# Operand tiles of a fused attention and two-FFN kernel begin 64 bytes further on than the weights' tiles

## The chip, the cores and the metric

One core of a Trainium2 chip runs one program. The metric is the device time of one execution in microseconds (us). The kernel before takes 951.75 us, the median of three runs (951.35 to 951.98).

## What is computed

```
scores = (q @ k^T) / sqrt(64) - log(448)        # 4 batches x 12 heads, 448 x 448 each, float32
attn   = sigmoid(scores) @ v
x      = attn, heads side by side               # 1792 tokens x 768
x      = (relu(x @ w_in)**2) @ w_out            # 768 -> 2048 -> 768
h      = x @ w_in2
out    = (h * sigmoid(1.702 * h)) @ w_out2      # 768 -> 2048 -> 768
```

All inputs and the output are float32.

## The kernel before, in words

There are two parts. In the first (until about 128 us) TensorE makes the scores of 24 pairs of heads and multiplies their sigmoids with v. Meanwhile ACT, DVE and the queue of POOL decode the four weight matrices: a step loads a raw block (`RAW`), turns it into float32 (`DEC`), adds and subtracts its quarters and writes seven blocks to DRAM (`scr`). Some of these steps are left to the second part, between its other work.

In the second part two token halves pass through the two FFNs: eight stages (`STAGES`), four of the kind "in" (`plan_in`) and four of the kind "out" (`plan_out`). Each stage is one Strassen-like product with seven partial products of eight units each, so 56 units. A unit is nine matmuls of 128 x 128 weights against 128 x 448 operand columns: three tiles in each of three passes, because a float32 factor is split into a high part that is rounded to fp32r and the low rest. The passes are high x high, high x low and low x high, lines 475 to 477. So the second part has 8 x 56 x 9 = 4032 matmuls, and each loads its own weights.

The weights of two units come by SP's queue into an `LD` tile; ACT copies its high part into an `SL` tile (named s), DVE subtracts to get the low part beside it. The operand of a partial product lies in a `T` tile (named t): `Operand` has ACT write the high half and DVE the low half. X, tmp and the four h tiles hold the matrices from which operands are made. The order on every engine is fixed when the program is built, by a planner (`settle`, `run`) with costs and due times of its own; a unit of TensorE counts there as `UNIT_US` = 1.8225 us.

The tiles of a pool lie one behind the other in SBUF, in the order in which they are asked for. Before the change this order is X (4 tiles of 5376 bytes in each partition), T (5 of 10752), LD (4 of 3072), SL (3 of 6144), tmp (5376), RAW (2 of 12288), DEC (2 of 6144), and then those of the attention (rq, qh, ql, rv, a, al, xst, bias, half), in whose place the h and sig tiles lie later. All sizes as far as the sig tiles, bias and half apart, are multiples of 256 bytes. So are all the offsets at which matmuls read within a tile: 512 bytes from one block of 128 weight columns to the next, 1536 and 3072 between the parts of an SL tile, 1792 and 5376 in a T tile. So the operand and the weights of every matmul of the second part begin at the same remainder of 256.

Of the kernel before, what the change touches and what calls it, by code (L numbers as in the profile page):

```python
# [9 lines left out]
F32R = mybir.dt.float32r  # L10
# [6 lines left out]
B, H, S, D = 4, 12, 448, 64  # L17
DM, DFF = 768, 2048
P = 128
# [10 lines left out]
NK = 3  # L30
# [5 lines left out]
NT = 5  # L36
# [42 lines left out]

PACE = (6, 6, 5, 1, 4, 5, 5)  # L80


@with_exitstack
def sigmoid_attention_two_ffn(ctx: ExitStack, tc: tile.TileContext, qk, v, w, outT):
# [13 lines left out]

    cpool = ctx.enter_context(tc.tile_pool(name="cpool", bufs=1))
    X = [[cpool.tile([P, NK, S], F32, name=f"xq{i}{j}") for j in range(2)] for i in range(2)]  # L100
    T = [cpool.tile([P, 2, NK, S], F32R, name=f"t{n}") for n in range(NT)]
    LD = [cpool.tile([P, 2, W], F32, name=f"ld{n}") for n in range(NLOAD)]
    SL = [cpool.tile([P, 2, 2, W], F32R, name=f"s{n}") for n in range(NSLOT)]
    tmp = cpool.tile([P, NK, S], F32, name="tmp")
    RAW = [cpool.tile([P, 4 * W, 2], U32, name=f"raw{n}") for n in range(2)]
    DEC = [cpool.tile([P, 4, W], F32, name=f"dec{n}") for n in range(2)]
# [30 lines left out]
    def act(fn, n, keys=(), after=(), extra=0.0, **kw):  # L137
        return Node("act", fn, 0.115 + extra + 0.833e-3 * n, keys, after, 0.105, **kw)
# [4 lines left out]
    def move(eng, out, in_, size, keys=(), after=(), **kw):  # L143

        def go():
            eng.dma_start(out() if callable(out) else out, in_() if callable(in_) else in_)

        n = Node("sp" if eng is nc.sync else "pool", go, 0.45 if eng is nc.sync else 0.55, keys, after, DMA_US + size / 250e3, **kw)
        n.size = size
        return n  # L150

    def activation(out, in_, fn=AF.Copy, **kw):
        nc.scalar.activation(out, in_, fn, **kw)  # L153
# [9 lines left out]
    def att_order():  # L163
        for u in range(NHP // 2 + 1):
            if u:
                yield from (("V", hp, c) for hp in (2 * u - 2, 2 * u - 1) for c in range(NFULL))
                yield ("VL", u - 1, 0)
            if u < NHP // 2:
                todo = [("S", hp, c) for hp in (2 * u, 2 * u + 1) for c in range(NFULL)]
                todo.insert(0 if u else NFULL, ("SL", u, 0))  # L170
                yield from todo
# [3 lines left out]
    def make_steps():  # L175
        kind = "L"
        us = {"S": SCORES_US, "V": VALUES_US, "VL": LEFT_US, "SL": LEFT_US}
        for key in att_order():
            new = "L" if key[0] in ("VL", "SL") else key[0]
            t = us["V" if key in WHOLE else key[0]]  # L180
# [61 lines left out]
    def load_qk(hp):  # L242
        if hp > 1:
            n = move(nc.sync, RQ[hp % 4], qk[hp], P * 2 * S * 4, (), [pe.get(("SL", (hp - 4) // 2, 0)), split.get(hp - 4)], part=0)
            rq_load[hp] = n, n
# [29 lines left out]
    def next_two():  # L275
        turn[0] += 1
        b = 2 * (turn[0] % 4)
        return b, mem["ps"][:, b : b + 2]
# [28 lines left out]
    def scores_left(u):  # L307
        b, ps = next_two()
        step = pe["SL", u, 0]

# [90 lines left out]
    class Operand:  # L401

        def __init__(self, src, n, keys, first, last):
# [3 lines left out]
            free_t[i] = last  # L407
            self.t = t = T[i]
            keys = [("T", i), *keys]
            act(lambda: activation(t[:, 0, : src().shape[1]], src()), n * S, keys, [units[old]] if old >= 0 else ())  # L410
# [38 lines left out]
    def plan_weights():  # L449
        for q in range(len(STAGES) * UNITS // 2):  # L450
            m, io, _ = STAGES[2 * q // UNITS]
            us = [ORDER[io][(2 * q + i) % UNITS] for i in range(2)]
            t, sl = LD[q % NLOAD], SL[q % NSLOT]
            ld = ("LD", q % NLOAD)
# [414 lines left out]
```

## Time and profile before

| | |
|---|---|
| median of three runs | 951.75 us |
| the profiled execution | 950.77 us |
| its span, first to last instruction | 949.0 us |
| matmuls in the second part | 4032 |
| first and last start of these | 128.06 and 945.09 us |
| granted TensorE clock | 1.00 throughout |

The page of the profile gives each engine's busy time, the chain of work that ended last, and the costliest groups of instructions by line. PE is TensorE's matmuls, PEld its weight loads. Matmuls overlap in their records: one is recorded from the time it starts until its last result is out, while the next has already started, so durations add up to more than the time. What a matmul costs is the distance from its start to the next one's.

### The profile page before, as it was taken

The numbers are of one execution on the slowest core, as the hardware profiler recorded it, in microseconds if no ns is written. First come the engines' busy times: TensorE is split into PE (matmuls) and PEld (weight loads), VectorE is DVE, ScalarE is ACT, GpSimd is POOL, SyncE is SP. The second block draws the span as 40 slices with busy tenths as digits, with TensorE's granted clock in tenths as the row PEclk, the third lists the DMA queues.
The fourth block names the chain that finished last, engine by engine and source line by source line (L and its number), as shares of the span: only waits on it lengthen the run. The fifth ranks groups of instructions, "written<-read, shape, count | busy, mean of one in ns | idle before, by whom it ended". The sixth has DMA issues, their size and how long they took to land.

```text
span 949.0 us, 13696 instructions
## 1 busy us (share of the span) xinstructions
PE 944.6 (100%) x4949; PEld 822.8 (87%) x4949; DVE 809.3 (85%) x839; ACT 604.6 (64%) x715; POOL 53.5 (6%) x100
## 2 busy tenths in 40 slices
PE   9999999999999999999999999999999999999998
PEld 4555479999999999999999999999999999999997
DVE  3989986699877999999999987999989999778662
ACT  6788776778868775555464666657684646445551
POOL 0110100000000000000000000000000000000000
PEclk9999999999999999999999999999999999999999
DMA  8899989999886766896567699877975448754341
GB/s 340 301 335 356 335 293 332 324 354 334 290 324 227 250 231 212 317 364 216 161 243 286 202 359 325 312 247 251 351 279 171 133 146 288 261 166 132 115 137 58
DMA packets 98627, 245.75 MB, mean 259 GB/s; under 512 B 10752, under 2 KB 72960, under 8 KB 94464
## 3 DMA queue, kind: packets, MB, share of 16 engines
q1 hardware_dynamic: 84736, 150.51, 46.5%
q0 software_dynamic: 13824, 94.38, 27.2%
q8 instruction: 38, 0.62, 0.3%
q14 instruction: 29, 0.24, 0.1%
HBM read 175.11 MB, written 69.73 MB: 258 GB/s over the span
## 4 chain that ended last, share of the span: by engine, by line
PE 100%; ACT 0%; issue 0%
PE ps L475 29%; PE ps L476 29%; PE ps L477 29%; PE ps L332 6%; PE ps L298 5%; PE ps L346 1%; PE ps L317 1%; PE ps L790 0%; PE ps L293 0%; ACT xq L635 0%; PE ps L471 0%
## 5 line engine op out<-in xcount | busy, mean ns | idle before, releaser
L475 PE MATMUL ps<-t,s 128*128 128x448 f32 x1344 | 490.9, 365 | 0.0
L477 PE MATMUL ps<-t,s 128*128 128x448 f32 x1344 | 490.8, 365 | 0.0
L476 PE MATMUL ps<-t,s 128*128 128x448 f32 x1344 | 490.8, 365 | 0.0
L153 ACT ACTIVATE s<-ld 128x768 fp32r<-128x768 f32 x224 | 189.4, 846 | 249.4 <-PE ps L476 206.6
L477 PEld LDWEIGHTS ps<-t,s 128*128 128x128 f32 x1344 | 252.5, 188 | 19.9
L476 PEld LDWEIGHTS ps<-t,s 128*128 128x128 f32 x1344 | 252.5, 188 | 19.9
L475 PEld LDWEIGHTS ps<-t,s 128*128 128x128 f32 x1344 | 252.5, 188 | 19.9
L156 DVE TENSOR_TENSOR s<-ld,s 128x768 fp32r<-128x768 f32 x224 | 213.6, 954 | 61.7 <-ACT s L153 56.6
L156 DVE TENSOR_TENSOR t<-h,t 128x1344 fp32r<-128x1344 f32 (+1 forms) x72 | 100.4, 1397 | 8.8 <-ACT t L153 8.7
L153 ACT ACTIVATE t<-h 128x1344 fp32r<-128x1344 f32 (+1 forms) x72 | 85.6, 1190 | 4.4 <-DVE h L156 2.9
L153 ACT ACTIVATE h<-ps 128x448 f32<-128x448 f32 x112 | 59.8, 536 | 27.0 <-PE ps L477 26.8
L153 ACT ACTIVATE a<-ps,bias 128x896 f32<-128x896 f32 x72 | 66.1, 1023 | 3.2 <-PE ps L293 3.2
L332 PE MATMUL ps<-a,rv 128*64 128x448 f32 x288 | 56.8, 543 | 0.1
L217 DVE SCALAR_TENSOR_TENSOR dec<-raw,dec 128x1536 uint32<-128x1536 uint32 x32 | 56.2, 1755 | 0.5
L219 DVE SCALAR_TENSOR_TENSOR dec<-raw,dec 128x1536 uint32<-128x1536 uint32 x32 | 56.1, 1753 | 0.3
L153 ACT ACTIVATE dec<-raw 128x1536 f32<-128x1536 f32 x32 | 51.9, 1621 | 0.0
L156 DVE TENSOR_TENSOR h<-h,h 128x1344 f32<-128x1344 f32 (+1 forms) x36 | 50.0, 1397 | 1.0 <-DMA h<-hm 0.8
L153 ACT ACTIVATE h<-h 128x896 f32<-128x896 f32 x48 | 44.9, 945 | 4.8 <-DVE h L156 4.4
L332 PEld LDWEIGHTS ps<-a,rv 128*64 128x64 f32 x288 | 19.6, 137 | 32.4 <-issue 22.6
L213 DVE TENSOR_SCALAR dec<-dec 128x1536 f32<-128x1536 f32 x32 | 30.7, 959 | 15.6 <-ACT dec L153 15.6
L156 DVE TENSOR_TENSOR t<-xq,t 128x1344 fp32r<-128x1344 f32 x24 | 37.2, 1552 | 5.9 <-ACT t L153 5.4
L156 DVE TENSOR_TENSOR h<-ps,h 128x448 f32<-128x448 f32 x64 | 38.8, 619 | 2.8 <-PE ps L477 2.5
(58 smaller groups left out, 616.1 us busy)
## 6 DMA issues: line engine op xcount, KB each, us to landing
ld<-scr SPq DMA_DIRECT2D x448, 192.0 KB, 3.8
raw<-in_w POOLq DMA_DIRECT2D x32, 1536.0 KB, 8.2
scr<-dec POOLq DMA_DIRECT2D x32, 768.0 KB, 5.5
scr<-raw POOLq DMA_DIRECT2D x28, 576.0 KB, 6.2
hm<-h SPq DMA_DIRECT2D x32, 448.0 KB, 5.8
h<-hm SPq DMA_DIRECT2D x16, 672.0 KB, 5.4
rq<-in_qk SPq DMA_DIRECT2D x22, 448.0 KB, 8.2
rv<-in_v SPq DMA_DIRECT2D x12, 448.0 KB, 6.1
```

Source lines behind the costliest of these rows:

```text
L153: nc.scalar.activation(out, in_, fn, **kw)
L156: nc.vector.tensor_tensor(out=out, in0=in0, in1=in1, op=op)
L213: dve(lambda: nc.vector.tensor_scalar(out=d, in0=d, scalar1=LEAST, scalar2=LARGEST, op0=ALU.max, op1=ALU.min), 4 * W, [dk], each=0.52e-3)
L217: dve(lambda: nc.vector.scalar_tensor_tensor(out=u, in0=raw[:, :, 0], scalar=29, in1=u, op0=ALU.logical_shift_right, op1=ALU.bitwise_or), ...
L219: dve(lambda: nc.vector.scalar_tensor_tensor(out=u, in0=raw[:, :, 1], scalar=0x80000000, in1=u, op0=ALU.bitwise_and, op1=ALU.bitwise_or), ...
L298: nc.tensor.matmul(ps[:, j, :S], kk[rows, keys], qq[rows, QUERIES], start=(i == 0), stop=(i == 2))
L317: nc.tensor.matmul(ps[out, j, :S], r[rows, :LEFT], r[rows, QUERIES], start=True, stop=True)
L332: nc.tensor.matmul(ps[rows, :S], t[:, hp % 2 * NFULL + c, rows], a[:, j], start=(c == 0), stop=False)
L346: nc.tensor.matmul(mem["ps"][out, b + i, :S], t[rows, 2 * NFULL, out], AL[rows, j], start=False, stop=True)
L475: nc.tensor.matmul(o, sh[:, cols], t[:, 0, k], start=start, stop=False, skip_group_check=True)
L476: nc.tensor.matmul(o, sh[:, cols], t[:, 1, k], start=False, stop=False, skip_group_check=True)
L477: nc.tensor.matmul(o, lo[:, cols], t[:, 0, k], start=False, stop=stop, skip_group_check=True)
```

## The change

The LD and SL tiles are asked for ahead of the T tiles. The first T tile gets 16 elements (64 bytes) more than it needs, and its operand begins behind them; the other four follow it without a gap. Each T is then a view of the same shape as before. So X, LD and SL keep the remainder of 256 at which they began, and everything from T on (tmp, RAW, DEC, the attention's tiles, h and sig) begins 64 bytes further on by that measure. No instruction, wait or transfer is added, removed or given another size. The planner's costs stay as they are.

```diff
+APART = 16
+
...
     X = [[cpool.tile([P, NK, S], F32, name=f"xq{i}{j}") for j in range(2)] for i in range(2)]
-    T = [cpool.tile([P, 2, NK, S], F32R, name=f"t{n}") for n in range(NT)]
     LD = [cpool.tile([P, 2, W], F32, name=f"ld{n}") for n in range(NLOAD)]
     SL = [cpool.tile([P, 2, 2, W], F32R, name=f"s{n}") for n in range(NSLOT)]
+    T = []
+    for n in range(NT):
+        skip = 0 if n else APART
+        t = cpool.tile([P, skip + 2 * NK * S], F32R, name=f"t{n}")
+        T.append(t[:, skip:].rearrange("p (a k n) -> p a k n", a=2, k=NK))
     tmp = cpool.tile([P, NK, S], F32, name="tmp")
```

## Rows read from the trace of the kernel before

**Rows 1.** The page: busy us of each engine (share of the span) x instructions.
```profile
PE 944.6 (100%) x4949; PEld 822.8 (87%) x4949; DVE 809.3 (85%) x839; ACT 604.6 (64%) x715; POOL 53.5 (6%) x100
```
**Rows 2.** The page: granted TensorE clock, in tenths, in 40 slices of the span.
```profile
PEclk9999999999999999999999999999999999999999
```
**Rows 3.** The page: chain that ended last, share of the span by line.
```profile
PE ps L475 29%; PE ps L476 29%; PE ps L477 29%; PE ps L332 6%; PE ps L298 5%; PE ps L346 1%; PE ps L317 1%; PE ps L790 0%; PE ps L293 0%; ACT xq L635 0%; PE ps L471 0%
```
**Rows 4.** Waits of PE: engine, line, releaser: us in total, times, longest.
```profile
PE ps L790 <- PEq L858: 0.8, 1, 0.8
```
**Rows 5.** Stretches: length, busy us (x) of PE, PEld, DVE, ACT, POOL; clock, DMA share.
```profile
130.00:240.00 110.00, 110.00 (x544) 101.97 (x543) 91.52 (x101) 78.80 (x105) 8.81 (x17) 1.00 0.91 320
240.00:340.00 100.00, 100.00 (x495) 92.68 (x494) 84.19 (x94) 78.08 (x104) 9.17 (x17) 1.00 0.80 283
340.00:440.00 100.00, 100.00 (x495) 92.70 (x494) 96.92 (x90) 58.36 (x59) 3.20 (x6) 1.00 0.79 280
440.00:540.00 100.00, 100.00 (x495) 92.68 (x495) 95.15 (x91) 54.95 (x56) 6.13 (x11) 1.00 0.63 209
540.00:640.00 100.00, 100.00 (x495) 92.70 (x494) 89.33 (x100) 64.33 (x86) 7.00 (x14) 1.00 0.88 311
640.00:740.00 100.00, 100.00 (x496) 92.68 (x495) 93.93 (x108) 63.18 (x87) 7.60 (x13) 1.00 0.74 260
740.00:840.00 100.00, 100.00 (x495) 92.69 (x494) 90.35 (x81) 55.33 (x59) 0.00 (x0) 1.00 0.61 203
840.00:949.00 109.00, 105.46 (x521) 97.40 (x519) 62.87 (x55) 47.91 (x51) 0.00 (x0) 1.00 0.36 118
```
**Rows 6.** Timeline of PE: the first and the last matmul of the second part.
```profile
128.06 0.45 PE L475 MATMUL ps<-t,s 128*128 128x448 f32 x1
...
945.09 0.37 PE L477 MATMUL ps<-t,s 128*128 128x448 f32 x1
```
**Rows 7.** Timeline of PE: six matmuls in a row, from 299.8 us.
```profile
299.80 0.36 PE L476 MATMUL ps<-t,s 128*128 128x448 f32 x1
300.00 0.37 PE L477 MATMUL ps<-t,s 128*128 128x448 f32 x1
300.20 0.36 PE L475 MATMUL ps<-t,s 128*128 128x448 f32 x1
300.41 0.36 PE L476 MATMUL ps<-t,s 128*128 128x448 f32 x1
300.61 0.36 PE L477 MATMUL ps<-t,s 128*128 128x448 f32 x1
300.81 0.36 PE L475 MATMUL ps<-t,s 128*128 128x448 f32 x1
```
**Rows 8.** Line 475: durations in ns (min/median/max), first and last start in us.
```profile
L475 PEld LDWEIGHTS ps<-t,s x1344: 187/188/203, 128.0 to 944.5; 128*128 128x128 f32 x192
L475 PE MATMUL ps<-t,s x1344: 362/365/447, 128.1 to 944.7; 128*128 128x448 f32 x192
```
**Rows 9.** Groups by shape, 300.19 to 300.3 us: a slow matmul (mean ns).
```profile
L477 PE MATMUL ps<-t,s 128*128 128x448 f32 x1 | 0.4, 369 | 0.0
```
**Rows 10.** The same at 40.05, 50.31 and 945.08 us: matmuls that no weight load follows.
```profile
L298 PE MATMUL ps<-qh,ql 64*128 64x448 f32 x2 | 0.4, 357 | 0.0
...
L298 PE MATMUL ps<-qh,ql 64*128 64x448 f32 x2 | 0.4, 364 | 0.0
...
L477 PE MATMUL ps<-t,s 128*128 128x448 f32 x1 | 0.4, 368 | 0.0
```
**Rows 11.** Timeline from 40.0 us: weight loads around the float32 matmuls of line 332.
```profile
40.09 0.36 PE L298 MATMUL ps<-qh,ql 64*128 64x448 f32 x2
...
40.45 0.20 PEld L332 LDWEIGHTS ps<-a,rv 128*64 128x64 f32 x4 [0.38 <-ACT a L153]
...
40.88 0.14 PEld L332 LDWEIGHTS ps<-a,rv 128*64 128x64 f32 x2 [0.23 <-issue]
41.26 0.14 PEld L332 LDWEIGHTS ps<-a,rv 128*64 128x64 f32 x2 [0.23 <-issue]
41.63 0.14 PEld L332 LDWEIGHTS ps<-a,rv 128*64 128x64 f32 x2 [0.23 <-issue]
```
**Rows 12.** Waits of all engines: the longest two on DMA outside POOL's queue.
```profile
DVE qh L261 <- DMA rq<-in_qk: 13.2, 5, 5.2
...
ACT s L153 <- DMA ld<-scr: 4.4, 2, 2.8
```

## The prediction

> **What bounds the kernel now.** I read the page's busy times first, then the chain, then PE's waits, then the stretches, and last the single matmuls. PE is busy for 944.6 of 949.0 us [rows 1], and the chain that ended last is PE almost alone: 87% of the span is lines 475 to 477, the second part [rows 3]. A busy PE proves little where matmuls overlap, so the waits must confirm it: PE's one wait is 0.8 us at the start [rows 4]. From 130 to 840 us each 100 us hold 495 or 496 matmuls, whatever the others do: DVE goes from 84 to 97 us, ACT from 55 to 78, the DMA share from 0.61 to 0.88 [rows 5]. So PE sets the pace, and its pace does not depend on the load on SBUF from other engines or from DMA.
>
> The pace itself: the last matmul starts 945.09 - 128.06 = 817.03 us after the first [rows 6], over 4031 distances, so 202.7 ns each; singly they are 0.20 or 0.21 us [rows 7]. The granted clock is full everywhere [rows 2], the 2.4 GHz level, at which 448 columns are 448 / 2.4 = 186.7 ns. So 16.0 ns of every matmul, 64 us in all, is something else. This change can act only there.
>
> The sum for the profiled execution: 128.06 us until the second part, 817.03 us of distances, 3.9 us from the last start to the end of the span, 1.8 us around the span: 950.8 us. The median of the runs is 1.0 us (0.1%) above it; I count changes from the median.
>
> **The change part by part.** It adds no instruction and no wait. What it can alter is the price of reading or writing an address.
>
> *Attention (128 us).* Its tiles all shift by the same 64 bytes, so weights and operand of its matmuls stay at equal remainders. 0 us. What hides a dearer access elsewhere in this part is that PE does not wait [rows 4].
>
> *ACT and DVE.* They write the same number of elements into t and s. A dearer write costs nothing while DVE has room: 84 to 97 us in 100 [rows 5]. The cover is thinnest from 340 to 540 us (192.1 of 200): from 4% more there, DVE would be late. I see no reason for even 1%, and take 0.
>
> *DMA.* Every transfer keeps its size; those of raw, dec, h, rq and rv begin 64 bytes off. The weight loads (`ld`) do not move. Waits for a DMA outside POOL's queue are 13.2 us on rq (DVE) and 4.4 us on ld (ACT), and no time of either reaches PE [rows 12, 4]. If the transfers of rq became 3% longer, those waits would grow by 0.4 us, still hidden. 0 us.
>
> *The 4032 matmuls of the second part.* Here the operand goes from equal remainder to 64 bytes beyond the weights'. While a matmul streams its operand, the next one's weights are loaded: loads take 188 ns of the 202.7 [rows 8]. If the two readings stand in each other's way, and if that depends on the remainder, the price changes here. The trace holds no f32r matmul at another relation, so I bound it.
> - Below: the float32 matmuls of line 332 follow each other pairwise at 0.375 us [rows 11], which is two times 187.7 ns, 448 columns twice with 1 ns to spare. A matmul of the second part at that pace would save 15 ns.
> - Nearer: matmuls behind which no weight load comes. A recorded duration is the distance to the next start plus a constant: 365 ns goes with 202.7, so 162 [rows 8, 7]. Line 298's last pair before a change of kind has its next load only 0.36 us after its start [rows 11], and lasts 357 ns at one place and 364 at another [rows 10], which is 195 and 202 ns. The very last matmul, which has no load beside it, lasts 368 [rows 10], which is 206. So without a load a matmul is 8 ns cheaper to 3 ns dearer than the usual one, on the mean of these three 2 ns cheaper.
> - Above: the slowest regular matmul lasts 369 ns [rows 9], 4 ns over the usual.
>
> The nearest row is the last matmul: same line, same shape, same tiles, no load beside it, and not cheaper. That speaks for the 16 ns being a property of the f32r stream and not a collision with the weight load. I take 0 ns, with -15 and +4 as ends.
>
> The Trainium skill weighs on both sides. Its page "SBUF — State Buffer", section "Who interferes with whom", gives TensorE two SBUF read ports, one for the moving operand and one for the weights, independent of each other; by that the change is worth nothing. Its page "TensorE: Matmul & The Clock Gate", section "Back-to-back issue gap", gives a warm matmul N / 2.4 + 2.5 ns, 189.2 ns for 448 columns; the trace shows 202.7, so by that page 13.5 ns lie in something it does not count. Were that the collision, the sum would be 4032 x 13.5 = 54 us less, an estimate.
>
> Sum: 0 us, so 951.7 us.
>
> **The rivals.**
>
> *A, the forecast: no address effect.* 951.7 us. For it: the last matmul, and a pace that nothing else touches [rows 10, 5]. Against it: the distances are not all alike. Durations of 362, 365 and 369 ns occur at one line [rows 8, 9], that is 199.5, 202.7 and 206.5 ns. A pure stream has no reason to vary, two readers that get in each other's way have one.
>
> *B, part of the 16 ns is the collision and 64 bytes lessen it.* For it: that variation, and the 357 ns of a matmul without a load. Against it: 364 and 368 ns, also without one. Price: half way between 357 and 364, so 4.5 ns under 365, is 4032 x 4.5 = 18 us: 933.6 us. Its ends are 1 and 8 ns, so 948 to 919 us.
>
> *C, all of it is the collision.* At 187.7 ns PE needs 0.926 of its time. DVE then sets the pace where it is busier than that: taking the larger of the two in each stretch, the second part shrinks by 8.1, 7.4, 3.1, 4.8, 7.4, 6.1, 7.4 and 7.7 us [rows 5], 52 us: 900 us. For it: line 332. Against it: that is a float32 matmul with half the weight columns, and all three rows of matmuls without a load.
>
> *D, slower: 64 bytes apart is the worse relation.* Mechanism: at equal remainders the two streams begin in step and the load's reads fall between the operand's; shifted, they meet, and every matmul takes what the slowest of the cycle takes now, 206.7 ns. Place: lines 475 to 477. Price: 4 x 4032 = 16 us: 968 us. It passes the 0.2% mark from 0.5 ns a matmul on, because nothing covers PE. For it: durations of 369 ns exist. Against it: the last matmul again. A dearer start of an unevenly placed operand would look the same and is counted here.
>
> **How the numbers follow.** A 0.44, B 0.30, C 0.08, D 0.18. I keep more than half of the chance away from A because one reader's rows cannot exclude an effect that no row shows, and 0.5 ns in 202.7 is enough to be measured. A measurement of this kernel tells about 0.2% (1.9 us) from no change. So faster 0.38, same 0.44, slower 0.18. Time 951.7 us. Range: A alone is 950.5 to 953 us. B reaches down to 919; from 928 on most of it is held. C is left out. Of D, 966 us holds the part up to 3.5 ns. Left out are 0.08 of C, some 0.05 of B and some 0.06 of D, 0.19 in all.
>
> **What would show it.** Right: distances of 0.20 to 0.21 us with a mean of 202.7 ns, 495 matmuls in 100 us, weight loads at 188 ns, median matmul 365 ns, the first start of the second part at 128.06 us. B would show 506 matmuls in 100 us and a median near 360 ns; C 520 or more, with PE waiting for DVE's s or t between 340 and 540 us; D 484 and a median near 369. In B to D the three durations of the cycle change; if only their order changes and the mean stays, A stands. If the time moves while the distances stay, the step on DMA or on DVE was wrong, and PE's waits must show for what. If the attention's end moves, an absolute start matters and not the relation.

## The result, and the profile after

The changed kernel takes 941.01 us, the median of five runs (940.27 to 941.72), against 951.35 us (950.83 to 951.98) for the kernel before on the same chip: ratio 0.9891, 95% interval 0.9876 to 0.9905. It is 1.1% faster. The likeliest case of the prediction (no change) did not come. The time moved as case B had it (18 us less, with ends of 4 and 32), by 10.3 us.

Of the page of the changed kernel: PE is still busy throughout, DVE and ACT do the same work [rows 1].

```profile
PE 934.2 (100%) x4949; PEld 821.4 (88%) x4949; DVE 808.1 (86%) x839; ACT 604.3 (64%) x715; POOL 54.4 (6%) x100
```

The stretches, columns as in [rows 5]. 100 us hold 502 matmuls where they held 495 or 496 before, in every stretch of 100 us alike. From 340 to 440 us DVE is now busy for 98.2 of 100 us, and still PE waits for nothing: its only wait is the one at the start, as in [rows 4].

```profile
240.00:340.00 100.00, 100.00 (x502) 93.72 (x501) 85.56 (x96) 79.29 (x104) 9.11 (x16) 1.00 0.82 289
340.00:440.00 100.00, 100.00 (x502) 93.73 (x501) 98.20 (x90) 58.36 (x59) 3.19 (x6) 1.00 0.79 276
...
740.00:840.00 100.00, 100.00 (x502) 93.73 (x501) 88.46 (x79) 55.55 (x59) 0.00 (x0) 1.00 0.64 211
```
```profile
PE ps L796 <- PEq L864: 0.8, 1, 0.8
```

The timeline of PE: the first and the last matmul of the second part, as in [rows 6].

```profile
128.39 0.45 PE L481 MATMUL ps<-t,s 128*128 128x448 f32 x1
...
934.68 0.37 PE L483 MATMUL ps<-t,s 128*128 128x448 f32 x1
```

So the 4031 distances take 934.68 - 128.39 = 806.29 us, 200.0 ns each, where they took 817.03: 10.7 us less. The second part starts 0.3 us later, and the tail is as long as before. The difference is the whole gain: 10.4 us of span.

The three lines of the second part (475 to 477 before, now 481 to 483), durations in ns, as in [rows 8].

```profile
L481 PE MATMUL ps<-t,s x1344: 363/363/449, 128.4 to 934.3; 128*128 128x448 f32 x192
...
L482 PEld LDWEIGHTS ps<-t,s x1344: 187/187/192, 128.5 to 934.3; 128*128 128x128 f32 x192
L482 PE MATMUL ps<-t,s x1344: 360/360/367, 128.7 to 934.5; 128*128 128x448 f32 x192
...
L483 PE MATMUL ps<-t,s x1344: 362/362/368, 128.9 to 934.7; 128*128 128x448 f32 x192
```

Before, all three lines had the median 365, and apart from the first matmul the range from 362 to 369 ([rows 8] shows one of them). Now each line has a duration of its own that hardly varies. The starts, which the trace holds in whole ns, show why: before, the distances repeated with a cycle of five matmuls (on the mean 202.5, 202.5, 199.2, 206.7 and 202.5 ns, in all 1013.3), which runs across the three lines of a block; now they repeat with a cycle of three (200.9, 197.5 and 201.6, in all 600.0), which coincides with them. The last matmul, with no load beside it, is recorded with 368 ns again, as in [rows 10]:

```profile
L483 PE MATMUL ps<-t,s 128*128 128x448 f32 x1 | 0.4, 368 | 0.0
```

### The profile page after: what moved, and what is told of

It is laid out like the page before. It is cut to its first block, busy times and chain, and to the rows that moved or that the text cites. A ratio compares the mean times of both kernels' runs of the same rounds, so it can differ in the third digit from the quotient of the medians.

```text
span 938.6 us, 13696 instructions
## 1 busy us (share of the span) xinstructions
PE 934.2 (100%) x4949; PEld 821.4 (88%) x4949; DVE 808.1 (86%) x839; ACT 604.3 (64%) x715; POOL 54.4 (6%) x100
## 4 chain that ended last, share of the span: by engine, by line
PE 99%; DMA 0%; ACT 0%; issue 0%
PE ps L481 29%; PE ps L483 29%; PE ps L482 28%; PE ps L338 6%; PE ps L304 5%; PE ps L352 1%; PE ps L323 1%; DMA rq<-in_qk 0%; PE ps L299 0%; ACT xq L641 0%; PE ps L477 0%
## 5 line engine op out<-in xcount | busy, mean ns | idle before, releaser
L481 PEld LDWEIGHTS ps<-t,s 128*128 128x128 f32 x1344 | 252.3, 188 | 13.3
```

Source lines behind the costliest of these rows:

```text
L481: nc.tensor.matmul(o, sh[:, cols], t[:, 0, k], start=start, stop=False, skip_group_check=True)
```

## The experiments

Distances below are between starts of the second part's matmuls, the mean over the kernel unless something else is said. Line numbers shift by a few lines between kernels; the three lines are always those of the three passes. Each kernel but the first ran once, and what is read from it is mainly distances within its trace.

### Both shifted

The edit against the changed kernel:

```diff
-    LD = [cpool.tile([P, 2, W], F32, name=f"ld{n}") for n in range(NLOAD)]
+    LD = []
+    for n in range(NLOAD):
+        skip = 0 if n else APART
+        t = cpool.tile([P, skip + 2 * W], F32, name=f"ld{n}")
+        LD.append(t[:, skip:].rearrange("p (a n) -> p a n", a=2))
...
+    T = [cpool.tile([P, 2, NK, S], F32R, name=f"t{n}") for n in range(NT)]
```

> LD, SL and T tiles all begin 64 bytes further on than in the kernel before, so operands and weights are at equal remainders again, but both absolute starts are moved. Theory R (only the distance between operand and weights by remainder of 256 counts): the distance between matmuls of the second part is 202.7 ns as before, median duration 365 ns, 951 us. Theory S (the operand's own start counts, since a shifted start suits its stream better): 200.0 ns, 362 ns, 941 us.

951.66 us, ratio to before 0.9999 (0.9989 to 1.0009); 202.7 ns. The groups by line:

```profile
L481 PE MATMUL ps<-t,s 128*128 128x448 f32 x1344 | 491.0, 365 | 0.0
L482 PE MATMUL ps<-t,s 128*128 128x448 f32 x1344 | 490.9, 365 | 0.0
L483 PE MATMUL ps<-t,s 128*128 128x448 f32 x1344 | 490.9, 365 | 0.0
```

The T tiles lie at exactly the addresses that they have in the changed kernel, and so does everything behind them. The gain is gone, with the distances of before and their cycle of five. So neither the operand's own start nor another tile that moved made it: theory S (the operand's start alone) falls, R (its place against the weights) stands.

### Fifteen distances between operand and weights

One T tile after another gets its own distance, so that one run measures five of them. The three runs differ only in the list of what is skipped (in elements of 4 bytes, each on top of the ones before); this is the first one's, against the changed kernel:

```diff
-NLOAD = 4
+NLOAD = 3
...
-    for n in range(NT):
-        skip = 0 if n else APART
+    for n, skip in enumerate((0, 8, 8, 8, 8)):
```

> One kernel, five distances: the five T tiles begin 0, 32, 64, 96 and 128 bytes further on than the weights by remainders of 256 (tiles ta to te); the load buffer has three tiles instead of four to make room, so its total time is not compared. Theory R: ta gives 202.7 ns (365 in the records), tc 200.0 (362 to 363), and tb, td and te lie elsewhere, as the two readings meet more or less often. Theory S gives the same for ta and tc. Theory N (the gain of the change came from another tile that moved, such as tmp or h, and not from operand and weights): all five alike, 200 ns.

> As the scan before, with 16, 48, 160, 192 and 224 bytes (tiles ta to te). Theory R with banks of 64 bytes that repeat every 256: ta (16) near 202.7, tb (48) between 200.0 and 202.7, and 160 to 224 differ from each other; 192, one bank behind, is not like 64, one bank ahead. Theory N: all alike.

> The scan of five T tiles again, with 40, 56, 72, 80 and 112 bytes (tiles ta to te). Known so far: 32 gives 206.4, 48 gives 200.2, 64 gives 199.9, 96 gives 205.4. Theory R with a smooth valley: 56 and 72 at or under 200, 40 and 80 between 200 and 205, 112 between 203 and 206. If 16-byte steps count and nothing finer does, 40 equals 32 or 48, 56 equals 48 or 64, and 72 equals 64 or 80.

From the first of these runs, the middle line's groups by operand tile (ta is 0 bytes, tb 32, tc 64, td 96, te 128); the last number but one is the mean duration in ns:

```profile
L481 PE MATMUL ps<-tb,s 128*128 128x448 f32 x279 | 102.8, 368 | 0.0
...
L481 PE MATMUL ps<-td,s 128*128 128x448 f32 x273 | 100.2, 367 | 0.0
...
L481 PE MATMUL ps<-tc,s 128*128 128x448 f32 x270 | 97.4, 361 | 0.0
...
L481 PE MATMUL ps<-ta,s 128*128 128x448 f32 x264 | 96.6, 366 | 0.0
L481 PE MATMUL ps<-te,s 128*128 128x448 f32 x258 | 94.5, 366 | 0.0
```

Mean distances of those matmuls that have at least nine of the same tile before them and one behind (268 to 285 for each value). These stretches are short and need not have settled, so half a ns tells nothing: 0 bytes gives 203.2 here and 202.7 over a whole kernel.

| bytes | ns | bytes | ns | bytes | ns |
|---|---|---|---|---|---|
| 0 | 203.2 | 56 | 203.4 | 112 | 202.4 |
| 16 | 202.1 | 64 | 199.9 | 128 | 203.8 |
| 32 | 206.4 | 72 | 206.7 | 160 | 204.2 |
| 40 | 201.9 | 80 | 207.0 | 192 | 204.3 |
| 48 | 200.2 | 96 | 205.4 | 224 | 206.3 |

In these kernels the time is 955.2 to 958.9 us, with mean distances of 203.2 to 204.5 ns, since most values are worse than 0. Theory N is out: the tiles of one run differ. The spread from 199.9 to 207.0 ns would be 29 us over 4032 matmuls. 64 and 48 are the best of the fifteen and are not told apart; equal remainders are in the better half. The smooth valley of the third expectation is not there: 56, between 48 and 64, is 3 ns dearer than both, so a step of 8 bytes counts. I have no rule that gives these fifteen numbers. That the relation and not the operand's own place counts was tested at 64 bytes alone, by the run with both shifted; the other values are read in the same way. So the idea of four banks of 64 bytes is not shown, and case D of the prediction was a real possibility: 80 bytes would have cost what D priced.

### Shorter weight loads

The edit against the kernel before; the third run makes the same one in the changed kernel, and the second has 32 for 64.

```diff
-                cols = slice(c * P, (c + 1) * P)
-                o = mem["ps"][:, b, :S]
+                cols = slice(c * P, c * P + 64)
+                o = mem["ps"][:64, b, :S]
```

> The kernel before, but each matmul of the second part loads only 64 of its 128 weight columns and gives 64 output rows (half of the product is left out). Operands, their order and their 448 columns stay. Theory C (the 16.0 ns over 186.7 are the meeting of weight load and operand stream): half the load makes half of it, so 194 to 195 ns. Theory P (they are the f32r stream's own, as the prediction's case A has it): 202.7 ns still.

> The kernel before with 32 of the 128 weight columns loaded by each matmul of the second part (three quarters of the product are left out). With 64 columns the distance was 202.2 ns, so the excess over 186.7 does not follow the number of columns. Theory K (the meeting happens where the load and the stream begin, whatever the length of the load): 201 to 203 ns again. Theory C, weakened: a load this short leaves the stream alone, 190 to 195 ns.

> The changed kernel with 64 of 128 weight columns loaded (half of the product is left out). At equal remainders this gave 202.2 ns with half the load and with a quarter. Theory K (the beginnings meet, so the relation counts as much for a short load): 199.5 to 200.5 ns. If the relation counts only through the length of the load: 202.2 ns again, since the load is over in the first third of the stream in both.

Equal remainders, 64 columns: 202.2 ns. With 32 columns: 202.2 ns. The load's record falls from 188 ns [rows 8] to 133 to 135 and 108. The groups of the 64-column kernel between 240 and 340 us, and the loads of the 32-column kernel:

```profile
L475 PE MATMUL ps<-t,s 128*64 128x448 f32 x166 | 61.0, 367 | 0.0
L476 PE MATMUL ps<-t,s 128*64 128x448 f32 x165 | 59.8, 362 | 0.0
L477 PE MATMUL ps<-t,s 128*64 128x448 f32 x165 | 59.6, 361 | 0.0
...
L476 PEld LDWEIGHTS ps<-t,s 128*64 128x64 f32 x165 | 21.9, 133 | 11.1
```
```profile
L475 PEld LDWEIGHTS ps<-t,s 128*32 128x32 f32 x165 | 17.8, 108 | 16.0
```

Theory C falls: a load of a quarter of the columns takes away 0.5 of 16 ns. The last expectation's "first third of the stream" stands in no row: the load of 64 columns is recorded with 133 to 135 of 202 ns. The third run, 64 columns at 64 bytes distance, gives 201.5 ns, in a cycle of nine, neither the 200 of theory K nor the 202.2 of its rival. The stretch from 240 to 340 us holds 498 matmuls, between the 496 of 64 columns at equal remainders and the 502 of the changed kernel:

```profile
240.00:340.00 100.00, 100.00 (x498) 1.00 0.81 285
```

So the place of the two still counts with a short load, but for 0.7 ns instead of 2.7; at 64 bytes the shorter load is even 1.5 ns dearer than the full one.

### Fewer operand columns

The edit against the kernel before, cut at the right; the second run has 320 for 384.

```diff
-                o = mem["ps"][:, b, :S]
-                nc.tensor.matmul(o, sh[:, cols], t[:, 0, k], ...
+                o = mem["ps"][:, b, :384]
+                nc.tensor.matmul(o, sh[:, cols], t[:, 0, k, :384], ...
```

> The kernel before with 384 of the 448 operand columns in each matmul of the second part (one seventh of the output is left out); equal remainders, full weight loads. 384 columns at 2.4 GHz are 160.0 ns. Theory F (the excess is paid once per matmul): 160.0 + 16.0 = 176.0 ns. Theory V (it is paid per column, a stream that is slower than one column a cycle): 160.0 x 202.7 / 186.7 = 173.7 ns. Only distances inside units are compared, since DVE may become the bound between them.

> The kernel before with 320 operand columns per matmul (the other 128 are left out of the product). With 384 the settled distance was 173.3 ns, 13.3 over the 160.0 of the columns, where 448 columns have 16.0 over at equal remainders and 13.3 at 64. Theory F (a fixed price of about 13.3 per matmul, to which the relation can add): 133.3 + 13.3 = 146.7 ns, or a little more. Theory V (one twelfth more per column): 144.4 ns.

The stretch from the first to the last start of the longest run without a wait of PE, in the 384-column kernel (591 matmuls, so 590 distances) and in the 320-column kernel (285):

```profile
775.78:878.04 102.26, 102.26 (x591) 1.00 0.49 159
```
```profile
821.17:862.80 41.63, 41.63 (x285) 1.00 0.47 148
```

102.26 us / 590 = 173.3 ns and 41.64 us (to the last start, at 862.82) / 284 = 146.6 ns, 13.3 over 160.0 and over 133.3. The first came out below both theories, nearer V (173.7), and suggested the second, which decides for F with 13.3 instead of 16.0: V would be 144.4. So an f32r matmul here pays 13.3 ns with 320 and 384 columns, at equal remainders. With 448 columns it pays 13.3 at a distance of 64 bytes and 16.0 at equal remainders. So at equal remainders the 448 columns alone of the three pay the further 2.7 ns, and in the two shorter streams there is no cycle: once settled, the distances are 173 or 174 and 146 or 147 ns. No other place was tried with 320 or 384. At 2.4 GHz 13.3 ns are 32 periods; that is arithmetic and names no cause.

The loads of the 384-column kernel, each recorded with 187 or 188 ns:

```profile
819.98 0.19 PEld L476 LDWEIGHTS ps<-t,s 128*128 128x128 f32 x1
820.15 0.19 PEld L477 LDWEIGHTS ps<-t,s 128*128 128x128 f32 x1
```

They start 173 ns apart, and 147 with 320 columns. So the records of loads overlap like those of matmuls, and "188 ns of the 202.7" is not the share of the time that a load takes.

### The halves of the weights apart

Three edits of the changed kernel: the low halves of an SL tile 128 bytes on, the high halves 64 on, and the low halves 64 on. They differ in the numbers; this is the second one's:

```diff
-NLOAD = 4
+NLOAD = 3
...
+        t = cpool.tile([P, 1664], F32R, name=f"s{n}")
+        halves = t[:, 16 : 1648].rearrange("p (a m) -> p a m", a=2)[:, :, : 2 * W]
+        SL.append(halves.rearrange("p a (i n) -> p a i n", i=2))
```

> The changed kernel, with the low halves of the weights 128 bytes further on (and three load buffers to make room): the operand is 64 bytes beyond the high halves and 192 beyond the low ones, where the scan gave 204. Theory next (the operand's stream meets the load of the next matmul's weights): the distance that grows is that from a line-482 matmul, while the low half for line 483 is loaded; from 197.5 to 201 or more. Theory own (it meets its own weights): the distance from line 483 grows and that from 482 does not. If the relation to the low half did not count at all, the mean would stay 200.0.

> The changed kernel with three load buffers and the high halves of the weights moved 64 bytes on, so that operands are at equal remainder with the high halves and 64 beyond the low ones. Moving the low halves alone (to 192) changed nothing, so the theory that all weights count alike has fallen. Theory H (the relation to the high halves, which two of three matmuls load, decides): the mean goes from 200.0 back to 202 to 203 ns. Theory L (it was the place of the LD tiles, which moved with the weights in the run where both were shifted): 200.0 ns stays.

> The converse: high halves in place (operand 64 beyond them), low halves moved 64 on, so at equal remainder with the operand. Theory H without the low halves: 200.0 ns, as at 192. If the low halves count after all and 192 was a chance, 200.5 to 201.5 ns, and it is the distance from line 482 that grows (197.5 now).

The groups by line of the three kernels, in this order:

```profile
L485 PE MATMUL ps<-t,s 128*128 128x448 f32 x1344 | 488.0, 363 | 0.0
L487 PE MATMUL ps<-t,s 128*128 128x448 f32 x1344 | 487.1, 362 | 0.0
L486 PE MATMUL ps<-t,s 128*128 128x448 f32 x1344 | 483.8, 360 | 0.0
```
```profile
L485 PE MATMUL ps<-t,s 128*128 128x448 f32 x1344 | 491.3, 366 | 0.0
L487 PE MATMUL ps<-t,s 128*128 128x448 f32 x1344 | 489.2, 364 | 0.0
L486 PE MATMUL ps<-t,s 128*128 128x448 f32 x1344 | 489.2, 364 | 0.0
```
```profile
L487 PE MATMUL ps<-t,s 128*128 128x448 f32 x1344 | 488.7, 364 | 0.0
L486 PE MATMUL ps<-t,s 128*128 128x448 f32 x1344 | 488.7, 364 | 0.0
L485 PE MATMUL ps<-t,s 128*128 128x448 f32 x1344 | 487.1, 362 | 0.0
```

Low halves at 192: 200.0 ns, 940.47 us, line by line the changed kernel. High halves at equal remainder: 202.2 ns, 949.92 us. Low halves at equal remainder: 201.1 ns, 945.25 us, and the distance from the middle line, behind which the low half is loaded, grows from 197.5 to 201.3. So it is the place of the weights against the operand that counts, and not that of the LD tiles (L falls), and both halves count. But the shares do not add up (2.2 and 1.1 ns, together 3.3, against 2.7 for both), and 192 for the low half alone costs nothing where 192 for both cost 4 in the scan. Theory next has the 197.5 to 201.3 for it and the 192 against it; with the low halves at equal remainder the distances repeat every twelve matmuls, so a line's mean mixes several of them. Which load meets which stream is not settled.

## Why the prediction was right in its range and wrong in its likeliest case

**What bounds the kernel** held: PE alone, no wait, one pace. The gain is 4031 distances times 2.7 ns, and beside it only the start of the second part moved. The parts that were costed at nothing (ACT, DVE, DMA, the attention) cost nothing that can be told from the 0.3 us at the start, and that start lies between 128.06 and 128.76 us over all kernels, in no order of their layouts. DVE's cover, 192.1 of 200 us [rows 5], sufficed for the faster pace.

**The step that failed** is "The nearest row is the last matmul: same line, same shape, same tiles, no load beside it, and not cheaper", and with it "I take 0 ns". A duration was read as the distance plus 162 ns. For matmuls that another one follows that holds, to 2 ns. For the last one it does not: it is recorded with 368 ns in both kernels, while the distances fell from 202.7 to 200.0. So that row does not follow the pace of its stream, and could say nothing about the load beside it. Nor is its surplus fixed: the last matmul of the second scan's kernel is recorded with 360 ns. In place of the 0 ns the term measured 2.7 ns a matmul.

The pairs of line 298 without a load (357 and 364) were as weak a base. With loads behind them that line's durations run over the same range in the kernel before:

```profile
L298 PE MATMUL ps<-ql,qh x140: 355/362/366, 6.2 to 121.9; 64*128 64x448 f32 x140
```

The mean of the two, half way, gave B's 4.5 ns, and the change brought 2.7. That the time fell inside the range is owed to the room given to B, and that B's size came so near is luck. The row that pointed the right way was the one that the prediction named against its case A: durations that differ in a stream whose operands are all alike. B rested on it and was given 0.30 of the chance, and the number itself took nothing from it.

**The size.** C and the 15 ns below did not come. Of the 16.0 ns over the columns' 186.7, 13.3 are the same with 320, 384 and 448 columns, and at 448 columns 2.7 could be had by placing. What the 13.3 are stays open. They do not follow the load's length, since 32 weight columns cost as much as 128 to within 0.5 ns; that they are paid where a load and a stream begin is not excluded, as every one of these matmuls has a load. Nor is it shown that the float32 matmuls of line 332, the prediction's bound below, go without them [rows 11]: two of these start 6 ns apart and the next two 375.8 ns later, and "448 columns twice" is one reading of that.

**The two rules.** For f32r, each matmul with its own load, the distance here is N / 2.4 + 13.3 ns at three values of N. The Trainium skill's page "TensorE: Matmul & The Clock Gate", section "Back-to-back issue gap", has N / 2.4 + 2.5 ns, but for a matmul by itself, and says that in a stream of loads and matmuls both set the spacing. No run here shows an f32r matmul by itself. So the 13.5 ns that the prediction took from that figure were no measure of a collision, and of the 54 us none of the fifteen places gives more than the 10.7 us measured. The run with both shifted and the scan show distances from 199.9 to 207.0 ns by the operand's place against the weights'. The page "SBUF — State Buffer" of the Trainium skill, section "Who interferes with whom", makes the two read ports of TensorE independent; here the two readings are not independent in their effect on the pace. Whether it is at the ports that they meet, no run shows.

**What stays open:** the mechanism. The experiments show that the relation by remainder counts and that it acts through both halves of the weights. They do not show what is shared. A distance is not a property of its line: the cycle of five runs across the three lines, and with 64 and with 32 weight columns at equal remainders the same three means (205.0, 201.7 and 200.0 ns) come at the lines in shifted places. That each distance depends on how the one before ended would fit this; it is a reading, not something that was taken apart.

**A better version:** none is pointed to. The fifteen places have their best at 64 and 48 bytes, and 200.0 ns is 186.7 plus the 13.3 that no placing here has reduced.

## What to carry to other kernels

Where PE is the bound and its distance exceeds columns divided by the clock, look at the single distances: a cycle in a stream of equal matmuls can be a sign that something meets, though not of how much there is to gain, since the changed kernel has one too. Then try where operand and weights lie against each other by remainders of 256; one run with a different place for each buffer measures many values. A wrong place can cost more than the right one gains (207.0 and 199.9 ns against 202.7), and with 320 and 384 columns equal remainders already have the 13.3 ns that 448 columns have at their best place. Don't read the duration of a matmul that nothing follows as a distance, nor that of a load as the time that it takes from the others.

## What the runs showed of the hardware that was not expected

- Moving only where f32r operands lie against the weights changes a 448-column matmul from 199.9 to 207.0 ns, not monotonically; moving both together by 64 bytes changes nothing (202.7 and 202.7).
- An f32r matmul with its own load pays 13.3 ns beside its columns with 320 and 384 of them at equal remainders, and with 448 at 64 bytes; cutting its load from 128 to 32 weight columns at equal remainders gives 202.2 instead of 202.7.
- Recorded weight loads overlap: with 320 operand columns loads of 187 to 188 ns start 146.6 ns apart.
- The distances settle in exact cycles: with 448 columns five matmuls in 1013.3 ns at equal remainders, three in 600.0 at 64 bytes, nine with half a load at 64 bytes.
